# Start of an attention-and-feed-forward kernel: iotas ahead of the first queued load, two q copies on VectorE, one memset moved to GpSimd, two idle matmuls more

## The chip, the cores and the metric

One core of a Trainium2 chip. The metric is the device time of one execution in microseconds (us), lower is better. The engines are called PE (TensorE, matmuls), PEld (its weight loads), DVE (VectorE), ACT (ScalarE), Pool (GpSimd) and SP (SyncE, which here only issues transfers). "L165" is line 165 of the kernel. Lines after the first moved load may stand lower or higher in a changed file: what is L351 before is L350 after.

## The reference, cut to what matters

```python
# q, k, v: (8, 8, 576, 64); moe_w_in (512, 2048), moe_w_out (2048, 512), all float32
k_p = k.reshape(B, H, Sp, 8, D).mean(axis=3)          # keys pooled by 8, Sp = 72
v_p = v.reshape(B, H, Sp, 8, D).mean(axis=3)
attn = softmax(scale * q @ k_p.T)                     # ... with 1e-9 in the denominator
x = (attn @ v_p) as (4608, 512) tokens
h = x @ w_in
out = (h * cos(h)) @ w_out
```

Eight batches of attention feed nine tiles of 512 tokens. Once the first tile is ready, the attention of later batches is worked into the gaps of the feed-forward matmuls, and PE hardly pauses again. Until then, the start, there is nothing to put into the gaps.

## The kernel before

The parts that the change touches. First the loads of batch 0. One half of k comes in float32 over the SP queue and is cast on ACT; all other loads go through the Pool queue, which casts to bf16 on the way. The iotas make a 0/1 matrix (`groups`) with which PE pools k and v by matmul.

```python
    EX = 5
    warm = consts.tile([128, 512], BF16, name="warm")
    nc.vector.memset(warm, 1.0)
    exp_tables()

    kv_even_tiles(0)
    q_tile(0)
    k_first = g_sb.rearrange("p f n -> p (f n)").bitcast(FP32)[:, 0:2 * ROW * D]
    nc.sync.dma_start(out=k_first.rearrange("p (j n) -> p j n", j=2), in_=even_view(k, 0, 0, 2))
    nc.scalar.copy(out=staged["k", 0][:, 0:2].rearrange("p j t d -> p (j t d)"), in_=k_first)
    load_even(staged["q", 0], 0, q, 0, 2)

    row_of = consts.tile([128, ROW], FP32, name="row_of")
    for rows in half:
        nc.gpsimd.iota(row_of[rows], pattern=[[1, ROW]], base=0, channel_multiplier=ROW,
                       allow_small_or_imprecise_dtypes=True)
    first_of = consts.tile([128, Sp], FP32, name="first_of")
    nc.gpsimd.iota(first_of, pattern=[[POOL, Sp]], base=0, channel_multiplier=0,
                   allow_small_or_imprecise_dtypes=True)
    load_even(staged["k", 0], 0, k, 2, 4)
    load_even(staged["q", 0], 0, q, 2, 4)
    load_even(staged["v", 0], 0, v)
    # ... identity, groups (three DVE instructions), constants
```

Then the other loads, in the order of the queue, and the idle matmuls:

```python
    kv_even_tiles(1)
    q_tile(1)
    for cg in range(3):
        load_w_in(cg)
    load_even(staged["k", 1], 1, k)
    load_even(staged["q", 1], 1, q, 0, 2)
    load_w_in(3)
    load_even(staged["q", 1], 1, q, 2, 4)
    load_w_out(0)
    load_even(staged["v", 1], 1, v)
    for i in range(2):
        nc.gpsimd.memset(kp2[i], 0.0)
    for cg in range(1, 4):
        load_w_out(cg)

    def warm_up(n, bank):

        for i in range(n):
            nc.tensor.matmul(bank, lhsT=warm[:, 0:128], rhs=warm)
```

The start itself, in program order. `scores` are PE matmuls and an exponential on ACT, `sums_first` PE matmuls and two activations, `values_then` PE matmuls and a DVE multiply into `xT`, `q_transpose_mm` PE transposes whose copy out of PSUM is done by the engine handed to it.

```python
    vec, act = nc.vector.tensor_copy, nc.scalar.copy
    us = BY_HEADS

    warm_up(10, obanks[0])
    pool_k_mm(0, obanks[1], 0, 2)(vec)
    warm_up(2, banks[1][:, 0, :])
    puts = q_transpose_mm(0, banks[2][:, 0, :], 0, 5), q_transpose_mm(0, obanks[0], 5, 9)
    puts[0](vec)
    puts[1](act)
    warm_up(2, banks[1][:, 0, :])
    scores(0, us[0], banks[0])
    scores(0, us[1], banks[1])
    pool_k_mm(0, obanks[1], 2, 4)(vec)
    sums_first(0, us[0], banks[0][:, 0, :])
    puts = q_transpose_mm(0, banks[2][:, 0, :], 9, 14), q_transpose_mm(0, obanks[0], 14, 18)
    puts[0](vec)
    puts[1](act)
    sums_first(0, us[1], obanks[1])
    scores(0, us[2], banks[0])
    scores(0, us[3], banks[2])
    nc.vector.memset(vz[1], float(POOL))
    pool_v_mm(0, banks[1])
    sums_first(0, us[2], obanks[0])
    values_then(0, us[0], obanks[1])
    values_then(0, us[1], banks[1][:, 0, :])
    sums_first(0, us[3], banks[2][:, 0, :])
    values_then(0, us[2], obanks[1])
    values_then(0, us[3], obanks[0])
    up_mm(0, 0, 0, 2)
    up_mm(0, 1, 0, 2)
    sin_tables()
    # ... t: tiles; in the down-projection of tile 0 the rest of batch 1's attention is slotted in
```

The pooling of v (L165 is its matmul, L167 its cast):

```python
    def pool_v_mm(b, pair):
        vb = staged["v", b]
        for t in range(ROW):
            for hp, rows in enumerate(half):
                nc.tensor.matmul(pair[:Sp, hp, 0:KCH * D], lhsT=groups[rows, t, :], rhs=vb[rows, :, t, :],
                                 start=(t == 0), stop=(t == ROW - 1))
        nc.vector.tensor_copy(out=v_part(b).rearrange("p j a d -> p a j d"),
                              in_=pair[:Sp, :, 0:KCH * D].rearrange("p a (j d) -> p a j d", j=KCH))
```

The softmax here doesn't subtract the row's maximum and nothing guards it: scores larger than these inputs give would overflow.

Of the kernel before, what the change touches and what calls it, by code (L numbers as in the profile page):

```python
# [14 lines left out]
POOL = 8  # L15
# [4 lines left out]
def kernel(  # L20
# [9 lines left out]
    nc = tc.nc  # L30
# [39 lines left out]
    vz = [wpool.tile([Sp, KCH, 4, D], BF16, name=f"vz{i}") for i in range(2)]  # L70

    banks = [psum.tile([128, 2, 512], FP32, name=f"bank{i}") for i in range(3)]
    obanks = [psum.tile([128, 512], FP32, name=f"obank{i}") for i in range(2)]
# [4 lines left out]
    staged = {}  # L78

    def even_view(src, b, j0=0, j1=KCH):  # L80
        return src[b, 2 * j0:2 * j1].rearrange("(j a) (p t) d -> (a p) j (t d)", a=2, t=ROW)

    def load_even(dst, b, src, j0=0, j1=KCH):
        nc.gpsimd.dma_start(out=dst[:, j0:j1].rearrange("p j t d -> p j (t d)"), in_=even_view(src, b, j0, j1))  # L84
# [31 lines left out]
    def load_w_out(cg):  # L116
        nc.gpsimd.dma_start(
            out=w_out_sb[cg],
            in_=moe_w_out[cg * 512:(cg + 1) * 512, :].rearrange("(f p) m -> p f m", p=128))
# [30 lines left out]
    def pool_k_mm(b, bank, pj0, pj1):  # L150

        kb = staged["k", b]
        ps = bank[:, 0:(pj1 - pj0) * Sp].rearrange("p (j n) -> p j n", n=Sp)
        for pj in range(pj0, pj1):
            for t in range(ROW):
                for rows in half:
                    nc.tensor.matmul(ps[rows, pj - pj0, :], lhsT=kb[rows, pj, t, :], rhs=groups[rows, t, :],
                                     start=(t == 0), stop=(t == ROW - 1))
        return lambda copy: put_kk(b, ps, pj0, pj1, copy)
# [9 lines that stand above are left out]
# [7 lines left out]
    def qT_tile(b):  # L176
        att["qT", b] = asb.tile([128, QB, 128], BF16, name="qT", tag="qT")

    def q_flat(b):
        return staged["q", b].rearrange("p j t d -> p (j t d)")  # L180
# [5 lines left out]
    def q_transpose_mm(b, bank, g0, g1):  # L186

        if ("qT", b) not in att:
            qT_tile(b)
        ps = bank.bitcast(BF16)[:, 0:(g1 - g0) * 128].rearrange("p (g n) -> p g n", n=128)  # L190
        for g in range(g0, g1):
            nc.tensor.matmul(ps[:, g - g0, :], q_flat(b)[:, g * 128:(g + 1) * 128], identity, is_transpose=True)
        return lambda copy: copy(out=att["qT", b][:, g0:g1, :], in_=ps)  # L193

    def ex_col(u, i):

        (c0, n), (h0, nh) = u
        return (i // 2 % 2 * (nh // 2) + i // 4 * 2 + i % 2) * n

    def scores(b, u, pair):  # L200
        scores_mm(b, u, pair)
        scores_exp(b, u, pair)

    def scores_mm(b, u, pair):
        (c0, n), (h0, nh) = u

        for i in [i + 2 * a for k in range(0, nh, 4) for i in (k, k + 1) for a in range(2)]:
            bank, c = divmod(ex_col(u, i), nh * n // 2)
            pj, hp = divmod(h0 + i, 2)
            g, r = divmod(ROW * pj + ORDER[c0 // 64], 2)  # L210
            nc.tensor.matmul(pair[:Sp, bank, c:c + n].rearrange("p (g n) -> p g n", n=64),  # L211
                             lhsT=kk[b % 2][half[r], h0 + i, 0:Sp],
                             rhs=att["qT", b][half[r], g:g + n // 64, hp * 64:hp * 64 + 64])

    def scores_exp(b, u, pair):
        (c0, n), (h0, nh) = u
        ex = asb.tile([Sp, 4 * 256], BF16, name="ex", tag="ex", bufs=EX)
        nc.scalar.activation(out=ex[:, 0:nh * n].rearrange("p (a n) -> p a n", a=2), in_=pair[:Sp, :, 0:nh * n // 2],  # L218
                             func=ACTF.Exp, scale=scale / POOL)
        att["ex", b, u] = ex  # L220
# [9 lines left out]
    def inverse_tile(w):  # L230
        lnc = asb.tile([128, 512], FP32, name="lnc", tag="lnc", bufs=1)
        inv = asb.tile([128, 512], FP32, name="inv", tag="inv", bufs=3)
        return lnc[:, 0:w], inv[:, 0:w]
# [26 lines left out]
    def sums_first(b, u, cs):  # L260

        (c0, n), (h0, nh) = u
        ex = att["ex", b, u]
        for i in range(nh):
            hp = i % 2
            nc.tensor.matmul(cs[hp * 64:hp * 64 + 64, (i // 2) * n:(i // 2 + 1) * n], lhsT=ones[:Sp, :],
                             rhs=ex[:, ex_col(u, i):ex_col(u, i) + n])
        w = nh * n // 2
        lnc, inv = inverse_tile(w)
        nc.scalar.activation(out=lnc, in_=cs[:, 0:w], func=ACTF.Ln)  # L270
        nc.scalar.activation(out=inv, in_=lnc, func=ACTF.Exp, scale=-1.0)
        att["inv", b, u] = inv
# [68 lines left out]
    k_first = g_sb.rearrange("p f n -> p (f n)").bitcast(FP32)[:, 0:2 * ROW * D]  # L341
    nc.sync.dma_start(out=k_first.rearrange("p (j n) -> p j n", j=2), in_=even_view(k, 0, 0, 2))
    nc.scalar.copy(out=staged["k", 0][:, 0:2].rearrange("p j t d -> p (j t d)"), in_=k_first)
    load_even(staged["q", 0], 0, q, 0, 2)

    row_of = consts.tile([128, ROW], FP32, name="row_of")
    for rows in half:
# [2 lines left out]
    first_of = consts.tile([128, Sp], FP32, name="first_of")  # L350
    nc.gpsimd.iota(first_of, pattern=[[POOL, Sp]], base=0, channel_multiplier=0,  # L351
                   allow_small_or_imprecise_dtypes=True)
    load_even(staged["k", 0], 0, k, 2, 4)
    load_even(staged["q", 0], 0, q, 2, 4)
    load_even(staged["v", 0], 0, v)
# [24 lines left out]
    load_even(staged["q", 1], 1, q, 2, 4)  # L380
    load_w_out(0)
    load_even(staged["v", 1], 1, v)
    for i in range(2):
        nc.gpsimd.memset(kp2[i], 0.0)  # L384
    for cg in range(1, 4):
# [2 lines left out]
# [6 lines that stand above are left out]
# [5 lines left out]
    puts = q_transpose_mm(0, banks[2][:, 0, :], 0, 5), q_transpose_mm(0, obanks[0], 5, 9)  # L399
# [4 lines left out]
    scores(0, us[1], banks[1])  # L404
    pool_k_mm(0, obanks[1], 2, 4)(vec)
    sums_first(0, us[0], banks[0][:, 0, :])
    puts = q_transpose_mm(0, banks[2][:, 0, :], 9, 14), q_transpose_mm(0, obanks[0], 14, 18)
    puts[0](vec)
    puts[1](act)
    sums_first(0, us[1], obanks[1])  # L410
    scores(0, us[2], banks[0])
    scores(0, us[3], banks[2])
    nc.vector.memset(vz[1], float(POOL))
    pool_v_mm(0, banks[1])
    sums_first(0, us[2], obanks[0])
    values_then(0, us[0], obanks[1])
# [8 lines left out]
    for t in range(NT):  # L425
# [5 lines left out]
        for fp in range(FFCH // 2):  # L431
            up_mm(t, fp, 2 if fp < 2 else 0)
            between = ()
            if t == 0:
                if fp == 4:
                    puts = pool_k_mm(1, obanks[0], 0, 2), pool_k_mm(1, obanks[1], 2, 4)
                elif fp in (5, 6):
                    g0 = 9 * (fp - 5)
                    puts = q_transpose_mm(1, obanks[0], g0, g0 + 5), q_transpose_mm(1, obanks[1], g0 + 5, g0 + 9)
# [95 lines left out]
```

## Time and profile before

| | before |
|---|---|
| three first runs, us | 302.48, 302.52, 302.74 |
| span in the profile | 300.7 us |
| PE busy | 293.3 us (98%) |
| first up-projection matmul (L297) | 17.17 us |
| PE waits for the second output weight | 0.29 us, ends at 37.84 |

A line of a timeline has the start, the time until the last of the group has ended, the engine, the line of code, the operation with its tiles, how many, and in brackets how long the engine was idle before it and what released it. The change moves work on DVE and ACT; these are the lines of it, first DVE before the change:

```profile
2.87 0.83 DVE L361 TENSOR_TENSOR dist<-row_of,first_of 128x648 f32<-128x648 f32 x1 [1.46 <-POOL first_of L351]
...
11.28 0.49 DVE L193 COPY qT<-bank 128x640 bf16<-128x640 bf16 x1
11.93 0.91 DVE L413 MEMSET vz<- 72x1024 bf16 x1 [0.16 <-issue]
14.56 0.69 DVE L167 CAST vz<-bank 72x512 bf16<-72x512 f32 x1 [1.72 <-ACT inv L271]
```

and ACT before:

```profile
12.04 0.57 ACT L193 COPY qT<-obank 128x512 bf16<-128x512 bf16 x1
```

DVE waits 1.46 us for the iotas and later has time to spare; ACT does the second late q copy only at 12.04, behind what is queued on it.

### The profile page before, as it was taken

What the parts mean: (1) busy time and instruction counts of PE and PEld (TensorE: products, weight loads), DVE (VectorE), ACT (ScalarE), POOL (GpSimd) and SP (SyncE); (2) the same over time, 40 slices, a digit from 0 to 9 for tenths busy, and PEclk for the clock granted to TensorE, in tenths of its full rate; (3) what the DMA queues carried; (4) which work ended last, traced back from release to release, by engine and by line L of the source; (5) the groups of instructions that cost most, each with busy time, mean ns of one, the idle gap of its engine ahead of it and who ended that gap; (6) DMA issues with size and microseconds to landing.
All of it is one profiled execution on the core that took longest, in us unless ns stands there. A gap on an engine that the chain in (4) does not pass through costs nothing.

```text
span 300.7 us, 4620 instructions
## 1 busy us (share of the span) xinstructions
PE 293.3 (98%) x1814; PEld 142.7 (47%) x1814; DVE 171.7 (57%) x212; ACT 206.1 (69%) x255; POOL 129.7 (43%) x92
## 2 busy tenths in 40 slices
PE   7899999999999999999999999999999999999995
PEld 3545544444544554445444544455445544444444
DVE  6558546574467446754675556654675477425712
ACT  3887897469866987688768886789668966605500
POOL 8553017985963497329913990389300000000000
PEclk9999999999999999999999999999999999999999
DMA  7999999729436951696079617791911130131023
GB/s 143 201 206 206 208 203 204 160 46 184 100 70 124 170 115 42 137 166 134 10 162 152 128 28 171 98 173 37 149 25 35 37 70 0 37 70 35 0 67 75
DMA packets 44166, 32.91 MB, mean 109 GB/s; under 512 B 22129, under 2 KB 39409, under 8 KB 44145
## 3 DMA queue, kind: packets, MB, share of 16 engines
q0 software_dynamic: 19744, 18.07, 38.3%
q1 hardware_dynamic: 24160, 14.42, 20.6%
q8 instruction: 14, 0.23, 0.3%
q10 hardware_dynamic: 240, 0.13, 0.2%
q14 instruction: 8, 0.06, 0.1%
HBM read 36.70 MB, written 9.44 MB: 153 GB/s over the span
## 4 chain that ended last, share of the span: by engine, by line
PE 86%; DMA 10%; POOL 2%; issue 0%; DVE 0%; POOLq 0%
PE obank L310 40%; PE bank L297 37%; DMA w_out_sb<-in_moe_w_out_dram 6%; PE bank L241 5%; DMA w_in_sb<-in_moe_w_in_dram 4%; PE bank L211 3%; PE bank L328 1%; POOL kv_st L84 1%; POOL kp L384 1%; POOL q_b L84 1%; POOL identity masks.py:197 0%; POOL row_of L348 0%; DVE o_sb L316 0%; POOL identity masks.py:199 0%; POOL first_of L351 0%
## 5 line engine op out<-in xcount | busy, mean ns | idle before, releaser
L310 PE MATMUL obank<-w_out_sb,g_sb 128*128 128x512 bf16 x560 | 131.4, 379 | 0.3 <-DMA w_out_sb<-in_moe_w_out_dram 0.3
L297 PE MATMUL bank<-xT,w_in_sb 128*128 128x512 bf16 x576 | 126.6, 379 | 0.0
L304 ACT ACTIVATE cos<-bank,half_pi 128x1024 f32<-128x1024 f32 x72 | 79.3, 1114 | 59.0 <-PE bank L297 59.0
L307 DVE TENSOR_TENSOR g_sb<-bank,cos 128x1024 bf16<-128x1024 f32 x72 | 87.3, 1223 | 42.6 <-ACT cos L304 42.5
L297 PEld LDWEIGHTS <-w_in_sb 128*128 128x128 bf16 x576 | 56.1, 98 | 67.6 <-issue 1.6
L310 PEld LDWEIGHTS <-g_sb 128*128 128x128 bf16 x560 | 52.8, 98 | 57.0 <-issue 2.5
L252 DVE TENSOR_TENSOR xT<-bank,inv 64x512 bf16<-64x512 f32 (+1 forms) x72 | 45.3, 629 | 41.2 <-ACT inv L248 40.5
L141 POOL TENSOR_TENSOR kv_st<-kv_st 72x2048 f32<-72x2048 bf16 x12 | 48.7, 4061 | 33.8 <-DMA kv_st<-in_k_dram 33.8
L247 ACT ACTIVATE lnc<-bank 64x512 f32<-64x512 f32 (+1 forms) x72 | 39.2, 544 | 3.3 <-PE bank L241 1.9
L316 DVE COPY o_sb<-obank 128x512 f32<-128x512 f32 x35 | 23.6, 689 | 31.1 <-PE obank L310 30.7
L218 ACT ACTIVATE ex<-bank 72x1024 bf16<-72x1024 f32 (+1 forms) x40 | 35.0, 929 | 8.7 <-PE bank L211 8.6
L142 POOL TENSOR_TENSOR kv_st<-kv_st 72x1024 f32<-72x1024 f32 x12 | 28.2, 2347 | 1.0
L248 ACT ACTIVATE inv<-lnc 128x512 f32<-128x512 f32 (+1 forms) x36 | 21.0, 583 | 1.1
L241 PE MATMUL bank<-ex,vz 72*128 72x256 bf16 (+1 forms) x176 | 20.0, 243 | 0.0
L241 PEld LDWEIGHTS <-vz 72*128 72x128 bf16 x176 | 13.6, 97 | 9.6 <-DVE xT L252 0.5
L145 POOL TENSOR_TENSOR kp<-kv_st 72x512 bf16<-72x512 f32 x12 | 14.9, 1265 | 0.5
L211 PE MATMUL bank<-qT,kk 64*72 64x256 bf16 (+1 forms) x192 | 13.3, 251 | 0.7 <-ACT qT L193 0.5
L211 PEld LDWEIGHTS <-kk 64*72 64x72 bf16 x192 | 7.6, 109 | 10.5 <-issue 7.7
L499 POOL COPY gate<-kk 1x1 bf16<-1x1 bf16 x5 | 0.9, 180 | 26.5 <-DMA kk<-kp 26.5
L285 ACT ACT_TABLE_LOAD x9 | 11.5, 1283 | 0.9 <-PEq L519 0.7
L288 ACT ACT_TABLE_LOAD x9 | 11.5, 1283 | 0.2
L84 POOL DMA_DIRECT2D q_b<-in_q_dram x10 | 7.7, 771 | 2.8 <-DMA w_in_sb<-in_moe_w_in_dram 1.4
(55 smaller groups left out, 89.4 us busy)
## 6 DMA issues: line engine op xcount, KB each, us to landing
out_dram<-o_sb SPq DMA_DIRECT2D x70, 128.0 KB, 2.4
kv_st<-in_v_dram POOLq DMA_DIRECT2D x8, 576.0 KB, 13.5
kv_st<-in_k_dram POOLq DMA_DIRECT2D x7, 576.0 KB, 7.6
q_b<-in_q_dram POOLq DMA_DIRECT2D x6, 576.0 KB, 9.7
w_in_sb<-in_moe_w_in_dram POOLq DMA_DIRECT2D x4, 512.0 KB, 13.4
w_out_sb<-in_moe_w_out_dram POOLq DMA_DIRECT2D x4, 512.0 KB, 18.5
q_b<-in_q_dram POOLq DMA_DIRECT2D x4, 288.0 KB, 12.0
g_sb<-in_k_dram SPq DMA_DIRECT2D x1, 576.0 KB, 3.6
```

Source lines behind the costliest of these rows:

```text
L141: add(out=s, in0=x[:, :, 0:4, :], in1=x[:, :, 4:8, :], op=ADD)
L142: add(out=s[:, :, 0:2, :], in0=s[:, :, 0:2, :], in1=s[:, :, 2:4, :], op=ADD)
L211: nc.tensor.matmul(pair[:Sp, bank, c:c + n].rearrange("p (g n) -> p g n", n=64), lhsT=kk[b % 2][half[r], h0 + i, 0:Sp], rhs=att["qT", b][h ...
L218: nc.scalar.activation(out=ex[:, 0:nh * n].rearrange("p (a n) -> p a n", a=2), in_=pair[:Sp, :, 0:nh * n // 2], func=ACTF.Exp, scale=scale ...
L241: nc.tensor.matmul(pair[:, hp, (i // 2) * n:(i // 2 + 1) * n], lhsT=vz[b % 2][:, pj, 2 * hp:2 * hp + 2, :].rearrange("p a d -> p (a d)"), ...
L247: nc.scalar.activation(out=lnc[half[1 - hp]], in_=pair[half[1 - hp], hp, 0:w], func=ACTF.Ln)
L252: nc.vector.tensor_mul(out=x_out(b, u, half[hp]), in0=cols(pair[half[hp], hp, :], u), in1=cols(inv[half[1 - hp]], u))
L297: nc.tensor.matmul(h[:, j, :], lhsT=w_in_sb[fc // 4][:, ki, (fc % 4) * 128:(fc % 4 + 1) * 128], rhs=xT[:, ki, t * TILE:(t + 1) * TILE], st ...
L304: nc.scalar.activation(out=cos, in_=h, func=ACTF.Sin, bias=half_pi[:, :1])
L307: nc.vector.tensor_mul(out=g_sb[:, 2 * fp:2 * fp + 2, :], in0=h, in1=cos)
L310: nc.tensor.matmul(o, lhsT=g_sb[:, fc, ms * 128:(ms + 1) * 128], rhs=w_out_sb[fc // 4][:, fc % 4, :], start=(fc == 0), stop=(fc == FFCH - 1))
L316: nc.vector.tensor_copy(out=o[:, 0:n], in_=ps)
```

## The change

Four moves. The iotas go ahead of the Pool queue's first load, so that DVE can make the mask sooner. The second late copy of q goes from ACT, which is full there, to DVE. To make room on DVE a memset of batch 1's value columns goes to Pool. Two idle matmuls fill the PE wait ahead of the third scores. The whole diff:

```diff
--- before.py
+++ after.py
@@ -341,7 +341,6 @@
     k_first = g_sb.rearrange("p f n -> p (f n)").bitcast(FP32)[:, 0:2 * ROW * D]
     nc.sync.dma_start(out=k_first.rearrange("p (j n) -> p j n", j=2), in_=even_view(k, 0, 0, 2))
     nc.scalar.copy(out=staged["k", 0][:, 0:2].rearrange("p j t d -> p (j t d)"), in_=k_first)
-    load_even(staged["q", 0], 0, q, 0, 2)
 
     row_of = consts.tile([128, ROW], FP32, name="row_of")
     for rows in half:
@@ -350,6 +349,7 @@
     first_of = consts.tile([128, Sp], FP32, name="first_of")
     nc.gpsimd.iota(first_of, pattern=[[POOL, Sp]], base=0, channel_multiplier=0,
                    allow_small_or_imprecise_dtypes=True)
+    load_even(staged["q", 0], 0, q, 0, 2)
     load_even(staged["k", 0], 0, k, 2, 4)
     load_even(staged["q", 0], 0, q, 2, 4)
     load_even(staged["v", 0], 0, v)
@@ -380,6 +380,7 @@
     load_even(staged["q", 1], 1, q, 2, 4)
     load_w_out(0)
     load_even(staged["v", 1], 1, v)
+    nc.gpsimd.memset(vz[1], float(POOL))
     for i in range(2):
         nc.gpsimd.memset(kp2[i], 0.0)
     for cg in range(1, 4):
@@ -404,13 +405,12 @@
     scores(0, us[1], banks[1])
     pool_k_mm(0, obanks[1], 2, 4)(vec)
     sums_first(0, us[0], banks[0][:, 0, :])
-    puts = q_transpose_mm(0, banks[2][:, 0, :], 9, 14), q_transpose_mm(0, obanks[0], 14, 18)
-    puts[0](vec)
-    puts[1](act)
+    for put in (q_transpose_mm(0, banks[2][:, 0, :], 9, 14), q_transpose_mm(0, obanks[0], 14, 18)):
+        put(vec)
     sums_first(0, us[1], obanks[1])
+    warm_up(2, banks[1][:, 0, :])
     scores(0, us[2], banks[0])
     scores(0, us[3], banks[2])
-    nc.vector.memset(vz[1], float(POOL))
     pool_v_mm(0, banks[1])
     sums_first(0, us[2], obanks[0])
     values_then(0, us[0], obanks[1])
```

## The prediction

> **What bounds the kernel now.** I read the page first: TensorE (PE) is busy 293.3 of 300.7 us, so only about 7.4 us of its idle time can be won at all. The windows view then says where that idle lies. Its columns are the stretch and its length, then each engine's busy time and instructions, then clock, DMA share (over 1 where packets overlap) and GB/s.
>
> ```profile
> 0.00:17.20 17.20, 13.61 (x171) 7.51 (x172) 10.28 (x22) 11.03 (x15) 10.80 (x22) 1.00 1.01 176
> 17.20:33.40 16.20, 16.20 (x154) 8.39 (x155) 11.60 (x15) 11.82 (x16) 5.99 (x8) 1.00 1.23 207
> 33.40:42.00 8.60, 8.31 (x72) 3.96 (x71) 3.15 (x6) 7.98 (x12) 0.84 (x1) 1.00 1.24 205
> 42.00:290.00 248.00, 247.96 (x1356) 117.98 (x1355) 144.28 (x167) 175.29 (x214) 112.12 (x62) 1.00 0.51 97
> ```
>
> PE idles 3.6 us in the first 17.2 us, 0.29 us between 33.4 and 42, and 0.04 us from there to 290. The change lies wholly in the first 20 us. So the question is only when the first up-projection matmul (L297) starts, 17.17 us now, and whether the one later wait, 0.29 us for an output weight, moves. I followed the start back through the timelines of PE, DVE and ACT. First PE:
>
> ```profile
> 5.83 0.77 PE L157 MATMUL obank<-groups,kv_st 64*64 64x72 bf16 x36
> 6.54 0.60 PE L391 MATMUL bank<-warm 128*128 128x512 bf16 x2
> 7.30 0.45 PE L192 MATMUL bank<-identity,q_b 128*128 128x128 bf16 x5 [0.16 <-DMA q_b<-in_q_dram]
> ...
> 12.66 0.59 PE L211 MATMUL bank<-qT,kk 64*72 64x256 bf16 x7 [0.54 <-ACT qT L193]
> 13.29 1.17 PE L165 MATMUL bank<-kv_st,groups 64*72 64x256 bf16 x18
> ...
> 16.57 0.63 PE L280 MATMUL obank<-ex,vz 72*64 72x256 bf16 x8 [0.42 <-DVE xT L282]
> 17.17 8.83 PE L297 MATMUL bank<-xT,w_in_sb 128*128 128x512 bf16 x40
> ...
> 37.84 0.81 PE L310 MATMUL obank<-w_out_sb,g_sb 128*128 128x512 bf16 x3 [0.29 <-DMA w_out_sb<-in_moe_w_out_dram]
> ```
>
> The columns are start, length, engine and line, and in brackets the idle time and what ended it. The first up-projection needs xT of two units, which two DVE multiplies finish at 17.11. They follow one another from 15.82, behind the value matmuls of 15.30, behind the DVE cast of the pooled v at 14.56, behind the pooling of v on PE (L165, 13.29 to 14.46). So the time is 13.29 + 3.88. What starts L165 at 13.29? Program order says the scores before it, which waited 0.54 us for a q copy on ACT. But the DMA says something else as well: the load of v was issued at 4.25 and takes 9.0 us to land (the DMA view of the first 8 us), that is 13.25; in the packet records the last completion write of v is at 13.15. For q the last one is at 7.17 and its first transpose at 7.30, the same 0.13 to 0.14 us later. So **two things end at once at 13.2: the scores, and the landing of v**. The second is the stream of Pool loads: first q half, second k half, second q half, v, then weights. From the first packet of q at 3.83 us (2.56 us after its issue at 1.27) the 16 DMA engines are saturated, and the same stream delivers the weight that PE waits for at 37.84:
>
> ```profile
> 19.36 18.43 DMA w_out_sb<-in_moe_w_out_dram
> 37.79 0.04 issue
> 37.84 0.81 PE obank L310 x3
> ```
>
> That is the chain of waits: start, length, what. After 37.84 PE never idles noticeably again before the tail. So **the end of the kernel is 37.84 plus fixed work, and 37.84 is set by when the load stream starts and how full it is kept**. Anything that makes PE reach this point sooner only lengthens the 0.29 us.
>
> **What the Trainium skill says.** "DMA: Bandwidth & Descriptors", section "Issuing engines are not separate DMA queues": loads from different issuers run on the same 16 engines and interleave. The trace agrees: k's first half (SP queue) has its packets from 2.09 to about 4.1, and the stream's share is then 0.94 to 1.25 per us until 18 us. The same page, "Anatomy of one DMA", gives a SWDGE load about 2 us of fixed cost; here 2.56 us pass from issue to first packet of the first q load. "SBUF — State Buffer", section "Who interferes with whom": a DVE instruction with at most one SBUF input, outside the two-port modes, does not contend with GpSimd. The xT multiplies have one input in PSUM and one in SBUF, so the moved memset should cost them nothing; no trace here shows it yet. "TensorE: Matmul & The Clock Gate", "What's actually happening": the array runs at half clock until busy for about 3.4 us. The trace agrees: the ten idle matmuls are 427 ns apart (4.43 us with the last one's drain), the later ones 216 ns.
>
> **The change, part by part.**
>
> 1. Iotas ahead of the first q load. On Pool:
>
> ```profile
> 1.27 0.87 POOL L84 DMA_DIRECT2D q_b<-in_q_dram  x1 [0.81 <-POOLq L519]
> 2.23 0.35 POOL L348 IOTA row_of<- 64x9 f32 x2
> 2.64 0.20 POOL L351 IOTA first_of<- 128x72 f32 x1
> 2.78 0.76 POOL L84 DMA_DIRECT2D kv_st<-in_k_dram  x1
> ```
>
> The iotas take 2.14 to 2.77, so 0.63 us with configuration. Swapped, DVE's three instructions on dist, sign and groups begin near 1.5 to 1.9 instead of 2.87 and end about 1 us earlier than 5.35. That wins nothing on PE: L157 needs also the cast of the first k half on ACT (4.42 + 1.15 = 5.57), and the ten idle matmuls, whose last streams until about 5.73. DVE's constants (5.51 to 6.50) come sooner, but the next DVE work waits for L157 at 6.6 anyway. The cost: q is issued up to 0.63 us later. From 0.65, when Pool passes the start barrier, to 1.27 it shows nothing; if the iotas run in that gap the delay is only about 0.2 us. I choose 0.2 to 0.63, middle 0.4. The later loads in the queue (2.78 on) are issued no later. How much of it the stream loses: k's first half leaves the engines at about 4.0 to 4.1, just when q's packets start (3.83). A q that starts at 4.2 to 4.5 leaves the engines a hole, less what they gain by clearing k faster. I estimate the stream is put back by 0.1 to 0.5 us, middle **0.25**. Then v lands at 13.5 and the weight at 38.05.
>
> 2. Late q copy (128x512) from ACT to DVE. On ACT it runs 12.04 to 12.61, behind four activations. On DVE it follows the copy that ends at 11.77; by the 0.49 us of the 640-column copy it takes about 0.4, ending near 12.2. The scores can go on 0.4 us sooner, at 12.25, and end near 12.9 instead of 13.25. ACT loses 0.57 us of a solid stretch (9.06 to 19.33), but what follows it, the first cosine at 19.95, waits for PE. The q delay of part 1 eats some of this. All of it ends in the wait for v: worth **0** while v lands at or after 13.2.
>
> 3. The value-columns memset, 0.91 us, leaves DVE at 11.93, where DVE was idle afterwards for 1.72 us: **0** there (it makes room for the q copy). On Pool it goes behind the v load of batch 1 (17.50) with about 0.9 us, by the 0.93 us of the neighbouring memsets of 80x1024. The next weight issue goes from 19.36 to 20.3; its packets queue for most of its 18.43 us behind others, so **0**.
>
> 4. Two idle matmuls: 2 x 216 ns = 0.43 us of PE, placed at about 11.75, where PE waits 0.54 us for the copy. The clock is granted in full already. Hidden by the wait for the copy or for v: **0 to 0.1**.
>
> Sum: +0.25 on the stream, 0 from the rest. 302.52 + 0.25 = 302.8; I write 302.7, as a slip into Pool's gap is a little likelier than the full delay.
>
> **The rivals.** (a) The q copy is the bound and v only happens to land then: L165 starts 0.4 us sooner, and the kernel ends 0.1 to 0.3 us sooner (the 0.29 us wait at 37.84 must absorb most of it): 302.2 to 302.4. For it: PE's wait is named ACT. Against: v's completion at 13.15. (b) Iotas fill the gap and the stream is not moved: 302.5. For it: 0.62 us of unexplained gap. (c) The stream loses the whole 0.63 us, and slow first packets add more: 303.1 to 303.3. For it: in the first 3 us the q packets move at half the later rate (48 per 0.5 us, later 90), with some of over 1 us. (d) The Pool memset delays an issue so that the stream runs dry: against it the backlog of 18 us.
>
> **Range and chances.** Between (a) and (c): 302.2 to 303.3. No path yields or costs 6 us, 2% of the time: the idle left is 7.4 us in all. Faster 0.005, same 0.99, slower 0.005.
>
> **What would show it.** In the new trace: q issue between 1.45 and 1.9, groups done near 4.4, first transposes of q at 7.5 to 7.8; both late copies on DVE, done by 12.5; PE idle just ahead of L165, ended by the DMA of v at 13.3 to 13.8; L297 3.88 us after L165; the weight at 37.9 to 38.3 and the wait there still present. The prediction is wrong if v lands sooner although q starts later, if L165 is not tied to v, or if the wait at 37.84 vanishes and PE alone sets the end.

A correction that the reader needs from here on: the times of single packets and completion writes in the prediction (2.09, 3.83, 7.17, 13.15 us), and those in the expectations below, were counted from a zero that lies 0.24 us before that of the timelines. Differences between two of them hold, differences to a timeline do not: the last completion write of v before the change came at 12.91, 0.38 us ahead of L165, not 0.14; and q's first packet (3.59) started 2.3 us after its issue, not 2.56. The last data packet of k's first half starts at 3.96, so q's packets and k's overlap, where the prediction has one hand over to the other. The landing of v at 13.25 is on the right zero: it is the sixteenth count of the load's semaphore, and it lies 0.04 us ahead of L165. So the reading that v ends at the same time as the scores stands. All packet times that I give from here on are on the timelines' zero.

## The result, and the profile after

| | before | after |
|---|---|---|
| runs of the first comparison, us | 302.48, 302.52, 302.74, 302.75 | 301.99, 302.07, 302.46, 303.21 |
| median | 302.63 | 302.26 |

The ratio is 0.9994 with a 95% interval of 0.9971 to 1.0017: the same. A ratio is the mean time of one kernel's fast runs over that of the other's of the same rounds, so not quite the ratio of the medians. The time lies in the predicted range, on the other side of "before" than predicted. What stands out is the scatter: the four runs of before lie within 0.27 us, those of after within 1.22 us. The profiled execution is the slowest of the four, 303.21 us, so its trace shows a bad draw, which is worth knowing before reading it.

The windows after, the stretches of the prediction (stretch, length, busy time and instructions of PE, PEld, DVE, ACT and Pool, clock, DMA share, GB/s):

```profile
17.20:33.40 16.20, 15.78 (x161) 8.31 (x157) 11.84 (x16) 11.64 (x16) 7.25 (x9) 1.00 1.23 207
33.40:42.00 8.60, 8.60 (x75) 4.10 (x73) 3.98 (x5) 7.81 (x12) 0.84 (x1) 1.00 1.24 205
42.00:290.00 248.00, 247.96 (x1359) 118.05 (x1356) 144.33 (x167) 176.14 (x216) 112.12 (x62) 1.00 0.51 96
```

PE is now full from 33.4 on: the 0.29 us wait is gone, because PE is late. The timeline of PE after says why:

```profile
5.85 1.29 PE L157 MATMUL obank<-groups,kv_st 64*64 64x72 bf16 x36
...
8.19 0.45 PE L192 MATMUL bank<-identity,q_b 128*128 128x128 bf16 x5 [0.49 <-DMA q_b<-in_q_dram]
...
12.54 0.61 PE L392 MATMUL bank<-warm 128*128 128x512 bf16 x2
13.07 0.63 PE L211 MATMUL bank<-qT,kk 64*72 64x256 bf16 x8
14.51 1.17 PE L165 MATMUL bank<-kv_st,groups 64*72 64x256 bf16 x18 [0.81 <-DMA kv_st<-in_v_dram]
...
18.38 8.83 PE L297 MATMUL bank<-xT,w_in_sb 128*128 128x512 bf16 x40
...
38.60 0.81 PE L310 MATMUL obank<-w_out_sb,g_sb 128*128 128x512 bf16 x3
```

(The 1.29 us of L157, 0.77 before, are a draw too: PE was granted its full clock from 7.16 us on here and from 5.75 on before, by the clock records of the two traces; the wait for q hid it.) The pooling of v starts at 14.51, after a wait for the landing of v that is now named outright, and L297 follows 3.87 us later, as 3.88 before. In the chain of waits after, 10.6 us of the path are the load of v:

```profile
3.85 10.62 DMA kv_st<-in_v_dram
14.47 0.04 issue
14.51 0.72 PE bank L165 x10
```

The same load took 9.0 us before. Yet the bulk of it was not late. The last data packet of v started at 12.82 us before; after, all but 14 of v's 512 data packets had started by then. The last 12 of these follow one another every 0.09 us from 13.06 to 14.04, as if one DMA engine were working off its share alone (the packet records don't name engines, so this is inferred). Each load ends with 16 completion writes, packets of 4 bytes; the last of v's came at 14.12, 1.1 us after the one before it (13.01). Before the change the last two came at 12.87 and 12.91. Pool and DVE after:

```profile
0.85 0.32 POOL L347 IOTA row_of<- 64x9 f32 x2 [0.39 <-POOLq L519]
1.24 0.20 POOL L350 IOTA first_of<- 128x72 f32 x1
1.42 0.88 POOL L84 DMA_DIRECT2D q_b<-in_q_dram  x1
2.29 0.73 POOL L84 DMA_DIRECT2D kv_st<-in_k_dram  x1
...
18.01 0.97 POOL L383 MEMSET vz<- 72x1024 bf16 x1
```

```profile
3.21 0.50 DVE L365 TENSOR_SCALAR groups<-sign 128x648 bf16<-128x648 f32 x1
...
12.58 0.41 DVE L193 COPY qT<-obank 128x512 bf16<-128x512 bf16 x1
...
18.30 1.29 DVE L282 TENSOR_TENSOR xT<-obank,inv 128x512 bf16<-128x512 f32 x2
```

The iotas cost the q load 0.15 us, not 0.63: they run where Pool had done nothing. The k load is issued 0.49 us sooner (2.29 against 2.78), and so are the ones behind it.

### The profile page after: what moved, and what is told of

It is laid out like the page before. It is cut to its first block, busy times and chain, and to the rows that moved or that the text cites. A ratio compares the mean times of both kernels' runs of the same rounds, so it can differ in the third digit from the quotient of the medians.

```text
span 301.4 us, 4625 instructions
## 1 busy us (share of the span) xinstructions
PE 293.9 (97%) x1816; PEld 143.2 (48%) x1816; DVE 170.8 (57%) x212; ACT 205.7 (68%) x254; POOL 130.4 (43%) x93
## 3 DMA queue, kind: packets, MB, share of 16 engines
q0 software_dynamic: 19744, 18.07, 38.3%
## 4 chain that ended last, share of the span: by engine, by line
PE 93%; DMA 4%; POOL 1%; DVE 1%; issue 0%; POOLq 0%; DVEq 0%
PE bank L297 41%; PE obank L310 41%; PE bank L241 5%; DMA kv_st<-in_v_dram 4%; PE bank L211 3%; PE bank L328 1%; PE bank L165 1%; POOL q_b L84 1%; PE obank L157 0%; PE obank L280 0%; PE obank L192 0%; DVE xT L282 0%; DVE vz L167 0%; POOL kv_st L84 0%; DVE o_sb L316 0%
## 5 line engine op out<-in xcount | busy, mean ns | idle before, releaser
L310 PE MATMUL obank<-w_out_sb,g_sb 128*128 128x512 bf16 x560 | 131.4, 379 | 0.0
L297 PE MATMUL bank<-xT,w_in_sb 128*128 128x512 bf16 x576 | 126.6, 379 | 0.0
L297 PEld LDWEIGHTS <-w_in_sb 128*128 128x128 bf16 x576 | 56.1, 98 | 67.6 <-issue 1.6
L310 PEld LDWEIGHTS <-g_sb 128*128 128x128 bf16 x560 | 52.8, 98 | 56.5 <-issue 2.0
L211 PE MATMUL bank<-qT,kk 64*72 64x256 bf16 (+1 forms) x192 | 13.2, 252 | 0.0
L103 POOL DMA_DIRECT2D kv_st<-in_v_dram x6 | 5.0, 841 | 8.8 <-PE bank L165 8.8
```

Of the source, the lines that this page charges most:

```text
L211: nc.tensor.matmul(pair[:Sp, bank, c:c + n].rearrange("p (g n) -> p g n", n=64), lhsT=kk[b % 2][half[r], h0 + i, 0:Sp], rhs=att["qT", b][h ...
L297: nc.tensor.matmul(h[:, j, :], lhsT=w_in_sb[fc // 4][:, ki, (fc % 4) * 128:(fc % 4 + 1) * 128], rhs=xT[:, ki, t * TILE:(t + 1) * TILE], st ...
L310: nc.tensor.matmul(o, lhsT=g_sb[:, fc, ms * 128:(ms + 1) * 128], rhs=w_out_sb[fc // 4][:, fc % 4, :], start=(fc == 0), stop=(fc == FFCH - 1))
```

## The experiments

Theory A: L165 cannot start before v has landed; the kernel's time is that start, plus fixed work, plus what PE still waits for the second output weight. The moves of the diff matter only through these. Rival B: the q copy on DVE is a steady gain of 0.4 us, and the landing of v is a coincidence. All results were correct. Times were compared on the same chip; intervals of the first four are wide because two of before's eleven runs there were slow ones of 306.26 and 304.18 us, at a mean clock of 0.982 and 0.993, of which more at the end. These four ratios are also too low; without the two they are 0.9992, 0.9993, 0.9996 and 0.9988, in the order below. I therefore read medians beside them, and call nothing shown that rests on 0.2 us of them.

**The change again**, and three parts of it.

> The changed kernel once more, for a second trace and a tighter ratio. Theory A (the start is set by the landing of batch 0's v, and the scatter of single runs is the scatter of that landing): ratio to before 0.998 to 1.000; in the trace the pooling of v (L165) starts 0.13 to 0.15 us after the last completion write of v, whatever that is, between 12.9 and 14.6 us; the iotas fit into Pool's gap, first q issue at 1.42. Rival B (the q copy on VectorE gives a steady 0.4 us): ratio 0.9985 or lower with L165 at or before 13.3 us and no wait for the DMA ahead of it.

Measured: 302.23 us median of 6 (302.00 to 302.72), before 302.63 of 11; ratio 0.9974 (0.9937 to 1.0011). That ratio lies under A's 0.998 and within B's range, but only through the two slow runs of before; without them it is 0.9992. B's other mark, no wait for the DMA, is not met. The profiled execution is again the slowest of its set. The PE timeline of this look:

```profile
11.99 0.63 PE L211 MATMUL bank<-qT,kk 64*72 64x256 bf16 x8
13.24 1.17 PE L165 MATMUL bank<-kv_st,groups 64*72 64x256 bf16 x18 [0.62 <-DMA kv_st<-in_v_dram]
...
38.16 0.81 PE L310 MATMUL obank<-w_out_sb,g_sb 128*128 128x512 bf16 x3 [0.66 <-DMA w_out_sb<-in_moe_w_out_dram]
```

Here PE has its scores behind it by 12.6 and stands before L165 for v; then it stands again for the weight. The two waits of theory A in one execution. The same kernel had L165 at 14.51 in the trace above: between two looks of one kernel, 1.3 us lie in the landing of v alone.

**The iotas alone.** Edit against before: only the first two hunks of the diff.

```diff
-    load_even(staged["q", 0], 0, q, 0, 2)
     row_of = consts.tile([128, ROW], FP32, name="row_of")
...
+    load_even(staged["q", 0], 0, q, 0, 2)
     load_even(staged["k", 0], 0, k, 2, 4)
```

> Before, with the iotas moved alone. Theory A: the q load starts 0.15 us later, the next loads 0.5 us sooner, and the load stream ends up level or 0.2 us ahead; v lands at 12.8 to 13.5; but the late q copy on ScalarE still holds L165 to 13.2 or later. Time 0 to 0.3 us under before. Rival B: the same as before or slower (302.6 to 302.9), since only the copy helps.

Measured: 302.50 us median of 6 (301.77 to 302.54), ratio 0.9975 (0.9938 to 1.0013).

```profile
12.57 0.59 PE L211 MATMUL bank<-qT,kk 64*72 64x256 bf16 x7 [0.54 <-ACT qT L193]
12.96 1.18 PE L165 MATMUL bank<-kv_st,groups 64*72 64x256 bf16 x18
...
37.89 0.81 PE L310 MATMUL obank<-w_out_sb,g_sb 128*128 128x512 bf16 x3 [0.53 <-DMA w_out_sb<-in_moe_w_out_dram]
```

v's last completion write came at 12.58 in this look, and L165 began at 12.96, 0.33 us sooner than before; still PE gained next to nothing: the wait for the weight grew from 0.29 to 0.53 us. I had expected the ACT copy to hold L165 to 13.2, but 12.96 came, because all of the start ran 0.1 us sooner; scores and v again came at the same time.

**The other three moves alone.** Edit against the change: the q load back ahead of the iotas.

```diff
+    load_even(staged["q", 0], 0, q, 0, 2)
     row_of = consts.tile([128, ROW], FP32, name="row_of")
...
-    load_even(staged["q", 0], 0, q, 0, 2)
     load_even(staged["k", 0], 0, k, 2, 4)
```

> The changed kernel with the iotas put back behind the first q load: so the copy, the memset and the two idle matmuls alone. Theory A: PE is ready for L165 at about 12.9 but v lands at 13.15 as in before, so PE waits for that DMA; time as before within 0.2 us. Rival B: 0.3 to 0.5 us under before.

Measured: 302.42 us median of 6 (302.11 to 302.79), ratio 0.9979 (0.9941 to 1.0016).

```profile
12.49 0.63 PE L211 MATMUL bank<-qT,kk 64*72 64x256 bf16 x8
13.30 1.17 PE L165 MATMUL bank<-kv_st,groups 64*72 64x256 bf16 x18 [0.18 <-DMA kv_st<-in_v_dram]
```

This answers the question between A and B in the trace: the copy on DVE lets the scores end sooner, and L165 starts at 13.30, as before at 13.29, because v lands when it did: last completion write at 12.93, before at 12.91. (The median is 0.21 us under before's, just over the 0.2 that A allowed.)

**Without the two idle matmuls.** Edit against the change:

```diff
     sums_first(0, us[1], obanks[1])
-    warm_up(2, banks[1][:, 0, :])
     scores(0, us[2], banks[0])
```

> The changed kernel without the two added idle matmuls. Both theories: within 0.15 us of the changed kernel, because they stand in a wait for the q copy. If they serve to hold the clock of TensorE, the up-projection matmuls that follow would be more than 216 ns apart here.

Measured: 302.18 us median of 6 (302.07 to 302.34), ratio 0.9971 (0.9930 to 1.0011). The same as the change within 0.05 us. The first up-projection takes 8.83 us here as in the change, so its clock was no lower. The two matmuls cost nothing and, in these six runs, give nothing.

**What puts the load stream ahead?** The prediction had the stream put back by 0.25 us. The packet records say the opposite: the 6000th data packet of the Pool queue starts at 37.03 us before and 36.83 in the kernel with the iotas back, but at 36.83, 36.65, 36.56 and 36.65 in the four looks with the iotas first (add 0.24 to compare with the expectations). Two edits against the change ask whether it is the sooner issue of the later loads (P) or DVE's mask work being out of the way (D).

```diff
     load_even(staged["q", 0], 0, q, 0, 2)
+    spare = consts.tile([128, 4, Sp], FP32, name="spare")
+    for i in range(4):
+        nc.gpsimd.iota(spare[:, i], ...)
```

> The changed kernel with four spare iotas on GpSimd between the first q load and the k load: q is issued at 1.42 as in the change, the k load and all after it at about 2.9, as late as in before. It asks why the load stream runs 0.25 us ahead with the iotas first (5 to 7 packets of over 600 ns in the first 8 us, against 11 and 12 in the two kernels with the iotas behind). Theory P (it is the later loads' earlier issue): 10 or more such packets, 6000th packet at 37.1 or later. Theory D (it is VectorE's mask work being out of the way): 5 to 7 packets, 36.8 to 37.0.

Measured, one look: 302.53 us (before 302.41 beside it); k load issued at 2.85; 5 long packets, 6000th packet at 36.85 (37.09 on the expectation's zero, 0.01 short of P's mark). The other puts DVE's three memsets of constants ahead of the three mask instructions:

```diff
+    nc.vector.memset(vz[0], float(POOL))
+    nc.vector.memset(ones, float(POOL))
+    nc.vector.memset(half_pi, math.pi / 2.0)
     nc.vector.tensor_tensor(out=dist, ...)
     nc.vector.scalar_tensor_tensor(out=sign, ...)
     nc.vector.tensor_scalar(out=groups, ...)
-    nc.vector.memset(vz[0], float(POOL))
-    nc.vector.memset(ones, float(POOL))
-    nc.vector.memset(half_pi, math.pi / 2.0)
```

> The changed kernel with VectorE's three constants ahead of its three mask instructions, so that the mask is made from about 2.5 to 4.9 us, nearly when before made it, with the loads issued as in the change. Theory P: 5 to 7 long packets and a 6000th packet at 36.8 to 37.0 as in the change. Theory D: 10 or more, 37.1 or later. The time itself stays within 0.5 us of the change either way.

Measured, one look: 301.83 us; 2 long packets, 6000th packet at 36.69 (36.93). So the lateness of the stream goes with the issue of the loads behind q (P) in both looks, and the count of long packets with neither theory: it was a bad marker. With overlapping values (36.83 in one look with the iotas first, 36.83 in one with them behind) and one look each, I take P as supported, not shown. Nor is this count what PE waits for: the weight landed at 37.70 and 37.19 in these two looks, but at 38.24 and 38.11 in the two looks at the change, whose 6000th packets were about as early. A stream can be ahead in packets while its last engine is behind.

**v later on purpose.** Edit against the change:

```diff
-    load_even(staged["v", 0], 0, v)
...
-    for cg in range(3):
-        load_w_in(cg)
+    load_w_in(0)
+    load_even(staged["v", 0], 0, v)
+    for cg in range(1, 3):
+        load_w_in(cg)
```

> The changed kernel with the load of v put behind the first weight load. Theory A: v lands 2.3 to 2.9 us later (512 KB more ahead of it), L165 starts at about 15.6 to 16.2 right after its last completion write, the first up-projection 3.88 us after that, there is no wait for the output weight, and the time is 304.2 to 305.2. Rival B (the scores and the q copy hold L165): the time moves by less than 0.5 us.

Measured, one look: 308.19 us at a mean clock of 0.981. PE, and then the windows:

```profile
16.10 2.14 PE L165 MATMUL bank<-kv_st,groups 64*72 64x256 bf16 x18 [3.22 <-DMA kv_st<-in_v_dram]
```

```profile
12.90:15.01 2.11, 0.00 (x0) 0.00 (x0) 0.00 (x0) 2.11 (x3) 0.77 (x1) 1.00 1.22 208
15.01:25.25 10.24, 8.66 (x50) 4.89 (x51) 3.31 (x5) 3.98 (x6) 5.64 (x7) 0.50 1.23 206
25.25:33.00 7.75, 7.75 (x84) 3.80 (x84) 4.86 (x5) 5.11 (x5) 1.61 (x2) 1.00 1.23 207
```

L165 follows v, 16.10 in the predicted 15.6 to 16.2, so the dependence is shown. The first up-projection came 5.47 us after it, not 3.88, and the time overshot the 304.2 to 305.2 by 3 us for a reason that I had not put in: with PE idle since 12.9, its clock fell to half at 15.01 and stayed there for 10.24 us, though work came back at 16.10. L165 takes 2.14 us instead of 1.17.

**v sooner on purpose.** Edit against the change: the first half of q also over the SP queue in float32, cast on DVE.

```diff
+    q_first = g_sb....bitcast(FP32)[:, 2 * ROW * D:4 * ROW * D]
+    nc.sync.dma_start(out=q_first..., in_=even_view(q, 0, 0, 2))
-    load_even(staged["q", 0], 0, q, 0, 2)
...
+    nc.vector.tensor_copy(out=staged["q", 0][:, 0:2]..., in_=q_first)
```

> The changed kernel with the first q half loaded by the SP queue in float32 behind k's first half and cast on VectorE, so that the Pool stream begins with k's second half and v lands about 1 us sooner. Theory A: q's first transpose at 6.8 to 7.2, L165 at 12.0 to 12.6, the first up-projection near 16.1, but the output weight still lands at 37.3 to 38.0 and PE waits 0.7 to 1.4 us for it: the time is 301.7 to 302.4, nearly all of the gain given back. Rival B (only the start counts): 301.0 to 301.4.

Measured, one look: 302.26 us. A miss in L165, 13.09 instead of 12.0 to 12.6. The bulk of v did come sooner: by 12.0 us only 7 of its data packets had not started, against 48 and 60 in the two looks at the change. But those 7 came one every 0.09 us until 12.61, as from one trailing engine, and the last two completion writes are at 12.04 and 12.70. The weight landed at 37.33, as expected, but PE was no earlier, so the expected wait did not come. The time lies in A's range without A's mechanism.

**Does the wait for the weight hide the gain?** All looks so far in one table. The last column is the time less the start of L165 less the wait for the weight.

| look | v's last write | L165 starts | PE waits for v | for the weight | time, us | rest |
|---|---|---|---|---|---|---|
| before | 12.91 | 13.29 | - | 0.29 | 302.51 | 288.93 |
| after | 14.12 | 14.51 | 0.81 | 0 | 303.21 | 288.70 |
| the change again | 12.84 | 13.24 | 0.62 | 0.66 | 302.72 | 288.82 |
| iotas alone | 12.58 | 12.96 | - | 0.53 | 302.47 | 288.98 |
| iotas back | 12.93 | 13.30 | 0.18 | 0.35 | 302.49 | 288.84 |
| no idle matmuls | 13.08 | 13.48 | 0.31 | 0 | 302.17 | 288.69 |
| spare iotas | 12.79 | 13.18 | - | 0.21 | 302.53 | 289.14 |
| constants first | 12.63 | 12.98 | 0.31 | 0 | 301.83 | 288.85 |
| q on SP | 12.70 | 13.09 | 0.28 | 0 | 302.26 | 289.17 |

A dash stands where the view names no wait. L165 starts 0.35 to 0.40 us after the last completion write of v in every one of the nine, with a dash or without, and 0.04 us after the sixteenth semaphore count. The rest is 288.7 to 289.2 everywhere, while L165 varies by 1.55 us: two landings, of v and of the weight, account for the time of each execution to 0.25 us. Both vary from run to run of one kernel. So I tried to take the second out: the weight loaded ahead of batch 1's v, and the pooling of that v later.

```diff
     load_w_out(0)
+    load_w_out(1)
     load_even(staged["v", 1], 1, v)
...
-            fill[1:] = [(2, S_(0, 0)), (8, lambda: pool_v_mm(1, banks[1])), (8, lambda: values(t, REST, banks[2])),
-                        (11, S_(1, 0)), (13, V_(0, 1)), ...
+            fill[1:] = [(2, S_(0, 0)), (8, lambda: values(t, REST, banks[2])), (11, S_(1, 0)),
+                        (14, lambda: pool_v_mm(1, banks[1])), (17, V_(0, 1)), ...
```

> The changed kernel with the second output weight loaded ahead of batch 1's v, and the pooling of that v moved six output matmuls later. It asks whether the wait for that weight (0.2 to 0.7 us in four of the runs so far) is what keeps the time from following L165. Theory A (time = start of L165 + about 288.8 us + that wait): the weight lands near 35.3, no wait for it, the time is 288.7 to 289.0 us above the start of L165, so 301.6 to 302.1 in the median, 0.2 to 0.5 us under the change. Rival B (the wait only moves to batch 1's v, as the same bytes must come): PE waits as long at the pooling of that v and the median stays at 302.2 to 302.4.

Measured: 303.74 us median of 5, ratio 1.0041 (1.0028 to 1.0054): 0.4% slower, clear of the noise.

```profile
36.56 0.39 PE L241 MATMUL bank<-ex,vz 72*128 72x64 bf16 x8 [0.58 <-ACT ex L218]
...
44.68 0.41 PE L211 MATMUL bank<-qT,kk 64*72 64x256 bf16 x4 [0.59 <-DVE xT L252]
```

The wait for the weight is gone, as A had it, but two waits of 0.6 us took its place: the pooling of v had been what PE did while ACT finished an exponential. They make up 1.2 of the 1.6 us by which this look's rest, 303.50 - 12.97 = 290.53, is above the table's. Neither theory had them. With the SP load of q on top (the edits of the last two diffs together) it was no different:

> Both: q's first half on the SP queue and the second output weight ahead of batch 1's v. Theory A: v lands at 12.9 to 13.3 as in the look at the first alone, no wait for the weight; 301.6 to 302.1 in the median and less scatter than the change, as fewer loads stand ahead of v in the Pool queue. Rival B: 302.2 to 302.4.

Measured: 303.66 us median of 5, ratio 1.0038 (1.0025 to 1.0051). A last try moved pieces again, with the weight loaded first as before:

```diff
-            fill[1:] = [(2, S_(0, 0)), (8, lambda: values(t, REST, banks[2])), (11, S_(1, 0)),
-                        (14, lambda: pool_v_mm(1, banks[1])), (17, V_(0, 1)), ... (26, S_(3, 1)),
+            fill[1:] = [(2, S_(0, 0)), (10, lambda: values(t, REST, banks[2])), (11, S_(1, 0)),
+                        (13, lambda: pool_v_mm(1, banks[1])), (16, V_(0, 1)), ... (28, S_(3, 1)),
```

> The second output weight ahead of batch 1's v once more, with the output stage rearranged so that the two 0.6 us waits that the first try made (for ScalarE ahead of the remainder's values, for VectorE ahead of the last scores) have other matmuls in front of them: values of the remainder at the 10th output matmul, pooling of v at the 13th, last scores at the 28th. Theory A: no wait for the weight, at most 0.3 us of new waits, time 288.8 to 289.2 us above the start of L165, median 301.8 to 302.2. Rival B (the stage of batch 1 has no slack, so any later pooling of its v costs as much as the wait for the weight did): 302.5 or more.

Measured: 303.64 us median of 5 (302.76 to 303.91), ratio 1.0037 (1.0023 to 1.0051). Of the two waits of 0.6 us, one of 0.30 us is left (for an exponential on ACT). Yet the rest, in the sense of the table, is 302.76 - 13.07 = 289.69 in this look, the fastest of the five, and some 0.8 us above the others: PE is idle 0.94 us between 33 and 42 us (9.00 less 8.06 busy), where the look with the constants first has 0.31. The view names only half of that. Rival B's time came: in the orders that I tried, that stage had no slack to pay with. Whether some other order has it stays open.

**The constants first, timed**, as the single look had been the fastest.

> The reordered VectorE constants again, timed. The single look gave 301.83 us. If that look was a lucky landing of v (12.98), the median is as the change's, 302.0 to 302.4; if the order of VectorE matters for the loads, 301.8 or under.

Measured: 302.41 us median of 5 (301.89 to 302.55), before 302.55; ratio 0.9998 (0.9984 to 1.0012). By the median the single look was a lucky draw. The look of this round (301.89) fits the table as a tenth line: L165 at 13.14, no wait for the weight, a rest of 288.75. No version beats the change clearly. Against before, one stands out once its two slow runs are left out: the change without the idle matmuls, whose six runs (302.07 to 302.34) have a mean 0.36 us under that of the nine (302.19 to 302.82), with a standard error of 0.08. It is one of four such comparisons, and was not run again.

## Why the prediction was right or wrong

**Right in range.** 302.26 us lies in 302.2 to 303.3, close to its lower end, and the difference is the small one that was given 0.99. The predicted sign, 0.2 us slower, did not come, and that the range held is in part luck: its middle rests on the stream term below, and single runs of the change span 301.99 to 303.21. Over all rounds the change has a median of 302.22 (10 runs), before 302.55 (33 runs), and the intervals of both comparisons hold 1.

- **"So two things end at once at 13.2: the scores, and the landing of v"**: shown, by the table above and by two experiments. With the copy moved, PE waits for v (iotas back: L165 at 13.30 as before); with v delayed, L165 follows it (16.10).
- **Part 1, "the stream is put back by 0.1 to 0.5 us, middle 0.25"**: the account behind this step failed. The iotas ran in Pool's gap between 0.65 and 1.27, so q was issued 0.15 us later, just below the 0.2 that I chose as the least. And I took the loads behind q as "issued no later" without counting that they would be issued 0.49 us sooner. Rival (b) had the gap right. By the count of packets the stream came out 0.2 to 0.5 us ahead of the look at before instead. By the landing that PE waits for, the size is neither confirmed nor refuted: the weight landed at 38.24 and 38.11 in the two looks at the change, within the predicted 37.9 to 38.3, but at 37.19 to 37.85 in the other five looks tabled with the iotas first, against 37.79 and 37.86 in the two with them behind. The scatter is larger than the term.
- **The signs it named**: L297 came 3.87 us after L165 in both looks at the change, as forecast. Of its three marks of being wrong, one came in each look and the third, an L165 not tied to v, in neither: v landed a little sooner although q started later (13.19 against 13.25, second look), and the wait at 37.84 was gone (first look). v itself landed at 14.47 and 13.19, on either side of the forecast 13.3 to 13.8.
- **Part 1, DVE's mask**: groups were done at 3.71, not near 4.4, since the iotas ended at 1.44; PE gained nothing from it, as said.
- **Part 2, the q copy**: 0.41 us on DVE, as estimated (0.4), and worth nothing while v lands at or after 13.2. Shown by the iotas put back.
- **Part 3, the memset**: 0.97 us on Pool against an estimated 0.9. The weight issued behind it moved from 19.36 to 20.69. That did not hold it up: it lands 2.53 to 2.61 us after the load ahead of it, batch 1's v, in all nine looks, with the memset there or not (2.59 before, 2.53 after). The two xT multiplies beside it (1.29 us for two) are no slower than their 0.69 each before, as "SBUF — State Buffer" has it.
- **Part 4, idle matmuls**: 0 to 0.1 us predicted, 0.05 between the medians, which is less than the scatter.
- **"The end of the kernel is 37.84 plus fixed work"**: right for most looks. In all nine, the time is the start of the L310 matmuls that need this weight plus 264.6 to 264.9 us. In seven they start 0.04 us after the weight has landed; in two of these seven (constants first, q on SP) PE arrived at the same moment, so no wait is named. In the other two PE came later than the weight: by 0.36 us after the change, because of v, and by 0.15 us without the idle matmuls. So the wait at 37.84 alone does not set the end; what comes last does, the weight or PE's own way from the landing of v. And I did not foresee that a landing scatters by over a microsecond between runs of one kernel.

**Open.** What the 0.3 us between the medians comes from: each half alone gave 302.4 to 302.5 and both together 302.2, as theory A would have it when v lands sooner and the scores are sooner too, but the intervals do not separate them. And whether the idle matmuls guard the clock: three of before's 33 runs took 304.2 to 307.3 us at a mean clock of 0.982 to 0.993, none of the 39 runs of kernels with the two matmuls at this place did (v put late left out), but none of the 12 runs of the two other kernels without them did either. An estimate from the run with v late: a stretch of 10.24 us at half clock takes 5.12 of 306 us, or 0.017, off the mean clock, about what the two slow runs at 0.982 lack. No trace of them was kept.

## What to carry to other kernels

When a stretch ends in two waits at the same time, a change that shortens one alone is worth nothing: look at the packet records of the load beside the wait that the profile names. Where a load stands in the stream that feeds the start decides when its work can begin, and a gap on the issuing engine is the place for small work. Read a single trace as one draw: here what looks like one trailing DMA engine moved a landing by 1.3 us, more than the whole change, so take several looks before telling a story of 0.5 us.

## What the Trainium skill lacked or had wrong

- "DMA: Bandwidth & Descriptors", "Why a DMA increments its semaphore by 16 and not by 1", says that only the full 16 means that all has landed. It does not tell how far the 16 lie apart: for the same v load the last completion write came at 12.84 in one look and 14.12 in another of the same kernel, and the last data packet started at 12.75 and 14.04.
- "TensorE: Matmul & The Clock Gate", "What's actually happening", puts the fall to half clock after an idle window of about 3.4 us. The section does not say what a partly busy stretch does. In the run with v late the clock fell after 2.1 us without a matmul, PE having worked 1.12 of the last 3.41 us, and stayed low for 10.24 us, of which PE was busy 8.66. The moment of the first full clock varies from run to run, as the section says, but by more than the 500 ns either way that it gives: 5.75 us before, 7.16 after, 4.77 (v late) and 7.34 (no idle matmuls) at the extremes, with the idle matmuls begun at 1.47 in each.
- No page has the gap of 0.62 us between the start barrier and the first load on the Pool queue (0.65 to 1.27); iotas put there started at 0.85, and the load then followed at 1.42 without a further gap.
